# Local attention and two MoE layers in one kernel: a new offline order from a planner whose model of the loads, due times and dummies are changed

## The chip, the cores and the metric

The kernel runs on one core of a Trainium2 chip. The time is the device time of one execution in microseconds, as the median of several runs; lower is better.

## What is computed

Attention in 16 heads (2 batches, 8 heads, 576 positions, 64 wide), each head once on means of four positions and once in a narrow band, and then two layers without experts' routing: the first with a rational function between its two products, the second with h x tanh(softplus(h)), which is Mish.

```python
q_d = q.reshape(B, H, Sd, factor, D).mean(axis=3)        # k_d, v_d likewise; factor 4
out_up = np.repeat(sm_attn(q_d, k_d, v_d), factor, axis=2)
mask = np.abs(pos[:, None] - pos[None, :]) < factor
out_local = softmax(np.where(mask, scale * q @ k.T, -1e9)) @ v
x = (out_up + out_local) -> [1152, 512]
h = x @ w_in                                             # 512 -> 2048, weights in float64
g = (a0 + a1 h + a2 h^2 + a3 h^3) / (1 + |b0||h| + |b1| h^2 + 1e-6)
x = g @ w_out                                            # 2048 -> 512
h = x @ w_in2;  out = (h * tanh(softplus(h))) @ w_out2
```

## The kernel before

The instructions are issued in an order that the program works out while it is built. `Plan.add` takes tasks: the engine or engines that may run one, its cost in microseconds, a due value (`prio`), what it waits for, and the buffers it takes and uses. `Plan.run` then plays the engines forward in time. A free engine takes the ready task with the least due value whose buffers are free, and calls its function, which emits the instructions. So the due values and the costs set only the order in which each engine's instructions stand in its queue. On the chip each queue runs in order, and semaphores hold it where data are missing. A number in the planner is no time of the chip.

Attention is cut into 18 units of 128 query rows of a pair of heads (`unit`; the last of each batch takes windows of four pairs and is called mixed). A unit has these tasks: the q load (`qload`, due value less LOFF), the v loads of its windows (`vload` in `unit`, L665, four DMAs, eight for a mixed one, due value plus VOFF, two buffers `vw`), transposes of q (`pe_a`, L552 as a helper's line), masked scores (`pe_b`, L712 to L728), maxima and exponentials on VectorE and ScalarE, transposes of the probabilities (`pe_d`), the products with v (`pe_e`, L827 and L837), and the writing of x as a high and a low part (`xhi`, `xlo`). Before the first unit of a pair of heads comes `prep`, with the k load (due value less KOFF), the load of v for the means (due value plus VROFF, L614), transposes, and sums on VectorE and POOL (L603, L620, L624). The units' due values start at PROL and rise by PSTEP in the first chunk; later chunks lie LEAD ahead of the layer's work that needs them; UOFF adds a number to each of the 18.

Weights come as 32 pieces ("grains") of 1 MB in float64, through two buffers `raw`. Their load (L994 for w_in, L999 for w_out) is due LLEAD ahead of use, their conversion CLEAD ahead: two ScalarE passes (L1011, L1018), a join on VectorE (L1025), a rounded high part (L1037) and a low part (L1042). OLAG puts the w_out pieces of the first layer later; GOFF adds a number to each of the first 12. The two small loads of a and b (L483, L484) have the fixed due value -34. All loads go through SP's queue, in the planned order.

The layers' work is done in steps of two blocks of 128 of the 2048 columns: products with w_in (L1155), the rational function (L1175 to L1254), products with w_out (L1288 in the first layer, L1290 in the second, whose first products are L1469 and L1525). The first group of the first layer works on chunks of 256, 256, 256 and 384 tokens, so that it can start when the first attention units are done.

Where TensorE has nothing ready in the planner, `fill` puts in a dummy product on zeros (`warm`, L533, 480 columns), if the share of work that the planner counts in a short look-back is under FILL. It occupies TensorE in the plan. It is emitted only while the plan's time lies in SHOW; outside, the plan leaves a hole of the same length. The planner models a load by the time that its issue takes on SP, at most eight at once, then 0.3 us, then its moving time behind the loads before it, then 1.1 us.

Of the kernel before, what the change touches and what calls it, by code (L numbers as in the profile page):

```python
# [25 lines left out]

SECOND = 1.8
COLD, FILL_ALL = 3.4, 20
WINDOW, FILL, FILL_END = 3.4, 0.9, 450.0
SHOW = (2.4, 30.0)  # L30
LEAD, CLEAD, LLEAD, OLAG = 38, 14, 40, 18
PROL, PSTEP, VOFF, VROFF, LOFF, KOFF = -45, 2.5, 2, -1, 7, 9
GROUPS = ([6, 6, 4], [4, 4, 4, 4])
KCUT, MIX = 4, (1, 4)
MKP = -45
# [3 lines left out]
NRAW, NWT, NRING, NRING2 = 2, 2, 3, (2, 1)  # L39
LAT = {"pe": 0.2, "act": 0.16, "dve": 0.15, "pool": 0.15, "sp": 1.1}  # L40
QUEUED = 8
UOFF = [-3.0, 0.0, 0.0, 3.0, 4.5, 3.0, 3.0, -1.5, 6.0, 0.0, 0.0, -4.5, -4.5, 4.5, 6.0, 4.5, -1.5, -1.5]
GOFF = [0.0, 0.0, 0.0, 0.0, -4.0, -4.0, -10.0, -6.0, 2.0, -4.0, 10.0, 12.0]
HP = 15


# [34 lines left out]
class Plan:  # L81
# [6 lines left out]
    def add(self, engs, fn, prio, after=(), take=(), use=(), chain=None, dens=0.5, port=False, dma=(), sub=None):  # L88
        t = Task()
        t.dma, t.sub = dma, sub  # L90
        t.port = port
        t.dens = dens
        t.engs, t.fn, t.prio, t.take = engs, fn, prio, list(take)
        t.out, t.next, t.started, t.ended, t.seq = [], None, False, False, len(self.tasks)
        t.use = list(take) + list(use)
        deps = set(after)
        for b in take:
            b.owner = t
        for b in use:
            deps.add(b.owner)  # L100
        for b in t.use:
            b.users += 1
        deps.discard(None)
        t.deps = len(deps)
        if chain is not None:
            if chain in self.last:
                self.last[chain].next = t
                t.deps += 1
            self.last[chain] = t
        for d in deps:  # L110
            d.out.append(t)
        self.tasks.append(t)
        return t

    def run(self, names):
# [3 lines left out]
        landed, moved = [0.0] * QUEUED, 0.0  # L119
# [15 lines left out]
        def free(s):  # L135
            freed.setdefault(s.space, {})[s.lo, s.hi] = now
# [11 lines left out]
        def place(t, e):  # L148

            for k in banks(t):  # L150
                if any(f != e and end > now + 1e-6 for f, end in touched.get(k, {}).items()):
                    return False
            got = []
            for b in t.take:
                for s in sorted(b.slots, key=age):
                    used = live.setdefault(s.space, {})
                    if s.gate is not None and not s.gate.ended:
                        continue
                    if any(f != e and end > now + 1e-6 for k in s.banks for f, end in touched.get(k, {}).items()):
                        continue  # L160
                    if all(s.hi <= o.lo or o.hi <= s.lo for o in used.values()):
                        b.slot = s
                        used[id(b)] = s
                        got.append(b)
                        break
                else:
                    for g in got:
                        del live[g.slot.space][id(g)]
                        g.slot = None
                    return False  # L170
            return True

        def fill():
# [7 lines left out]
            for s in slots:  # L181
                used = live.setdefault(s.space, {})
                if all(s.hi <= o.lo or o.hi <= s.lo for o in used.values()):
                    b = Buf(slots)
                    b.slot, b.users, used[id(b)] = s, 1, s
                    if SHOW[0] <= now < SHOW[1]:
                        shown = fns[-1](s.view)
# [8 lines left out]
        while True:  # L196
            for e in names:
                if until[e] > now:
                    continue
                held = []  # L200
                while ready[e]:
                    item = heapq.heappop(ready[e])
                    t = item[2]
                    if t.started:
                        continue
                    one = next(iter(t.engs))
                    if e != one and until[one] + t.engs[one] <= now + t.engs[e] + SECOND:
                        held.append(item)
                        continue
                    if not place(t, e):  # L210
                        held.append(item)
                        continue
                    t.started = True
                    t.fn(e) if len(t.engs) > 1 else t.fn()
                    begin = max(now, 0.65) if e == "sp" else now
                    if e == "pool" or e == "dve" and t.port:

                        begin = max(now, port[0])
                        port[0] = begin + t.engs[e]
                    end = until[e] = begin + t.engs[e] * (2 if e == "pe" and now < COLD else 1)  # L220
                    there = end + LAT[e]
                    if t.dma:
                        end = begin
                        for issue, move in t.dma:
                            end = max(end, landed[-QUEUED]) + issue
                            moved = max(moved, end + 0.3) + move
                            landed.append(moved + LAT["sp"])
                        until[e], there = end, landed[-1]
                    n += 1
                    heapq.heappush(events, (end, n, 0, e, t))  # L230
                    heapq.heappush(events, (there, n, 1, e, t))
                    for k in banks(t):
                        touched.setdefault(k, {})[e] = there
                    if t.next is not None:
                        t.next.deps -= 1
                        if not t.next.deps:
                            enable(t.next)
                    if e == "pe":
                        busy.append((now, end, t.dens))
                    break  # L240
                for item in held:
                    heapq.heappush(ready[e], item)
                if e == "pe" and until[e] <= now:
                    got = fill()
                    if got:
                        b, dur = got
                        end = until[e] = now + dur * (2 if now < COLD else 1)
                        busy.append((now, end, 1))
                        n += 1
                        heapq.heappush(events, (end, n, 2, e, b))  # L250
            if not events:
                break
            now = events[0][0]
            while events and events[0][0] <= now + 1e-9:
                _, _, kind, e, t = heapq.heappop(events)
                if kind == 0:
                    if e == "pe":
                        release(t, e, True)
                    continue
                if kind == 2:  # L260
                    del live[t.slot.space][id(t)]
                    continue
                t.ended = True
                done += 1
                for b in t.use:
                    b.users -= 1
                    if not b.users:
                        del live[b.slot.space][id(b)]
                        free(b.slot)
                release(t, e, False)  # L270
# [4 lines left out]
def kernel(  # L275
# [26 lines left out]
    add = plan.add  # L302
# [184 lines left out]
    t_id = add({"pool": 1.1}, lambda: make_identity(nc, ident), -1000)  # L487
    t_m = add({"dve": 0.1}, lambda: nc.vector.memset(band, 0.0), -1900)
    t_cd = add({"dve": 0.6}, zeros, -1000)
    add({"dve": 0.4}, lambda: None, -880)  # L490
    t_bn = add({"pool": 0.5}, bands, -900, after=[t_m])
    def mask_set(lo, hi, ws):
        for w in ws:
            masks(*w)
# [2 lines left out]
    t_mk = [  # L497
        add({"dve": cost}, lambda x=x: mask_set(*x), pr, after=[t_bn])
        for cost, pr, x in (
            (0.4, -890, (0, 4, ((0, 0, 1), (0, 1, 1), (0, 2, 1), (0, 3, 1)))), (0.25, MKP, (3, 7, ((1, 4, 4),))),  # L500
            (0.25, MKP, (7, 11, ((2, 8, 4),))),
        )
    ]
    t_bias = add({"pool": 0.1}, biases, -20)
# [129 lines left out]
    def unit(u, slots, start):  # L634
        bb, kind, wins, prio, nw, n = u.bb, u.kind, u.wins, u.prio, NW, 32 * NW
        pairs = sorted({p for p, _ in wins})
        mixed = len(pairs) > 1
# [68 lines left out]
        def pe_b():  # L706
# [24 lines left out]
                        )  # L731

        tb = add(
            {"pe": 1.6 if mixed else 0.86}, pe_b, prio,
            after=tq + [kv_done[p] for p in pairs] + [t_i16, t_mk[kind]],
            take=[sc, tm, s, pd],
            use=[qT] + mix, chain="pb",
# [157 lines left out]
    first = [(0, 256), (256, 256), (512, 256), (768, 384)]  # L895
# [57 lines left out]
    for c in range(4):  # L953
        for i, (bb, kind, p) in enumerate(need[c]):
            if c == 0:
                prio = PROL + PSTEP * i
            else:
                prio = cstart[c - 1] + (i / len(need[c])) * (cstart[c] - cstart[c - 1]) - LEAD
            prio += UOFF[len(att_order)]
            att_order.append(prio)  # L960
# [20 lines left out]
    for g in sorted(grains, key=lambda g: grains[g]):  # L981
        m, kind, f = g
        pr = grains[g] + (GOFF[len(W)] if len(W) < len(GOFF) else 0.0)
        r, t, w = Buf(raw_s), Buf(wt_s), Buf(ring_s[kind])
# [600 lines left out]
```

## Time and profile before

| what | value |
|---|---|
| median of 3 runs | 481.8 us (479.96 to 482.65) |
| the profiled execution: its time, and the span of its instructions | 481.31 us, 479.5 us |
| busy share of the span: TensorE, VectorE, ScalarE, POOL | 98%, 79%, 70%, 12% |
| mean granted clock of TensorE | 0.993 of full speed |
| loads and stores | 47.17 MB, 98 GB/s in the mean |
| instruction packets on queue 8 | 32, 0.52 MB, 0.5% of the time of 16 DMA engines |

The profile is of one execution. Busy time of an engine is the time covered by its instructions; a TensorE matmul overlaps the next one, so the step between two is shorter than the duration shown. Idle time is put down to what ended it. The granted clock is a share of full speed, and has two levels, 1.2 and 2.4 GHz.

### The profile page before, as it was taken

Reading aid. Unit: us, or ns where it says so; the run is one execution under the profiler, and the core shown is the slowest. Engines: PE = TensorE matmul, PEld = TensorE weight load, DVE = VectorE, ACT = ScalarE, POOL = GpSimd, SP = SyncE. Lnnn points to the kernel's source line nnn. Section 1 sums busy time; section 2 is a strip of 40 time slices with the busy share of each in tenths; the row PEclk is TensorE's granted clock in tenths of the full one; section 3 lists DMA queues with packets and bytes.
Section 4 is the critical chain, followed back from the end, with each engine's and each line's share of the span. In section 5 each row is a group of like instructions: output and inputs, shape, how many; then the busy total and the mean of one; then the engine's idle time right before and its main releaser. Section 6 shows DMA issues by size and latency. Waiting matters only on the chain.

```text
span 479.5 us, 9855 instructions
## 1 busy us (share of the span) xinstructions
PE 467.6 (98%) x4081; PEld 428.5 (89%) x4081; DVE 376.8 (79%) x566; ACT 337.6 (70%) x529; POOL 58.7 (12%) x80
## 2 busy tenths in 40 slices
PE   8999898999999999999999999999999999999996
PEld 4667797889999999999999998898989898989885
DVE  6688789899899978997999989988596669524342
ACT  5778698885988799998878797578667446422320
POOL 2654345653000000000000000000000000000000
PEclk9999799999999999999999999999999999999999
DMA  8967976611422402333022022134314220000103
GB/s 180 234 172 176 263 184 182 153 42 36 168 89 90 143 34 87 106 130 117 0 89 89 1 89 87 45 115 143 137 21 156 87 89 0 1 0 2 66 1 131
DMA packets 45757, 47.17 MB, mean 98 GB/s; under 512 B 30352, under 2 KB 31120, under 8 KB 45712
## 3 DMA queue, kind: packets, MB, share of 16 engines
q1 hardware_dynamic: 45712, 46.54, 33.4%
q8 instruction: 32, 0.52, 0.5%
q14 instruction: 13, 0.11, 0.1%
HBM read 44.17 MB, written 2.36 MB: 97 GB/s over the span
## 4 chain that ended last, share of the span: by engine, by line
PE 74%; DVE 12%; DMA 8%; ACT 3%; issue 1%; SPq 1%; ACTq 0%
PE psum L1290 19%; PE psum L1155 18%; PE psum L1288 15%; PE psum L1469 11%; PE psum L1525 5%; DMA att<-in_q_dram 3%; DMA raw<-in_moe_w_in_dram 3%; PE psum L837 1%; DMA att<-in_v_dram 1%; PE psum L827 1%; DVE wt L1025 1%; PE psum L552 1%; DVE xl L1311 1%; DVE wrk L1329 1%; PE psum L728 1%
## 5 line engine op out<-in xcount | busy, mean ns | idle before, releaser
L1155 PE MATMUL psum<-xh,wi 128*128 128x384 f32 (+1 forms) x336 | 84.7, 323 | 0.2 <-DVE wrk L1184 0.2
L1288 PE MATMUL psum<-gg,wo 128*128 128x384 f32 (+1 forms) x480 | 76.2, 313 | 0.0
L1288 PEld LDWEIGHTS psum<-gg,wo 128*128 128x128 f32 x480 | 72.8, 189 | 0.5 <-issue 0.2
L1155 PEld LDWEIGHTS psum<-xh,wi 128*128 128x128 f32 x336 | 60.2, 193 | 1.5 <-issue 0.9
L1155 PE MATMUL psum<-xl,wi 128*128 128x384 f32 (+1 forms) x168 | 53.1, 316 | 0.0
L1290 PE MATMUL psum<-wo,gg 128*128 128x512 f32 x216 | 51.7, 391 | 0.0
L1290 PE MATMUL psum<-wo,late_g 128*128 128x512 f32 x216 | 51.3, 391 | 0.0
L1290 PEld LDWEIGHTS psum<-wo,late_g 128*128 128x128 f32 x216 | 40.4, 188 | 8.0
L1290 PEld LDWEIGHTS psum<-wo,gg 128*128 128x128 f32 x216 | 40.4, 188 | 8.0
L1025 DVE SCALAR_TENSOR_TENSOR wt<-wt,raw 128x1024 int32<-128x1024 int32 x32 | 40.4, 1266 | 7.5 <-ACT wt L1011 6.5
L1011 ACT ACTIVATE wt<-raw 128x1024 f32<-128x1024 f32 x32 | 36.4, 1137 | 8.7 <-DVE wo L1042 4.8
L1018 ACT ACTIVATE raw<-raw 128x1024 int32<-128x1024 uint16 x32 | 36.8, 1149 | 4.7 <-DMA raw<-in_moe_w_out_dram 3.4
L1525 PE MATMUL psum<-xh,wi 128*128 128x384 f32 x128 | 34.5, 335 | 0.0
L1155 PEld LDWEIGHTS psum<-xl,wi 128*128 128x128 f32 x168 | 32.5, 193 | 0.0
L1401 DVE TENSOR_TENSOR part<-psum,part 128x512 f32<-128x512 f32 x27 | 17.8, 687 | 13.6 <-PE psum L1290 13.6
L1155 PE MATMUL psum<-xh,late_r 128*128 128x384 f32 x96 | 25.5, 334 | 0.0
L1175 ACT ACTIVATE wrk<-psum 128x768 f32<-128x768 f32 (+1 forms) x27 | 19.9, 735 | 6.6 <-PE psum L1155 6.0
L1037 ACT ACTIVATE wo<-wt 128x1024 fp32r<-128x1024 f32 x11 | 11.7, 1061 | 17.7 <-DVE wt L1031 7.7
L1042 DVE TENSOR_TENSOR wo<-wt,wo 128x1024 fp32r<-128x1024 f32 x14 | 17.1, 1218 | 8.7 <-ACT wo L1037 8.7
L1525 PEld LDWEIGHTS psum<-xh,wi 128*128 128x128 f32 x128 | 23.3, 188 | 0.2
L1099 ACT ACT_TABLE_LOAD x17 | 21.8, 1283 | 0.3
L1525 PE MATMUL psum<-xl,wi 128*128 128x384 f32 x64 | 21.4, 335 | 0.0
(164 smaller groups left out, 1038.5 us busy)
## 6 DMA issues: line engine op xcount, KB each, us to landing
raw<-in_moe_w_in_dram SPq DMA_DIRECT2D x16, 1024.0 KB, 5.4
raw<-in_moe_w_out_dram SPq DMA_DIRECT2D x16, 1024.0 KB, 4.9
att<-in_v_dram SPq DMA_DIRECT2D x72, 48.0 KB, 4.0
out_dram<-part SPq DMA_DIRECT2D x9, 256.0 KB, 2.0
att<-in_q_dram SPq DMA_DIRECT2D x16, 128.0 KB, 3.9
att<-in_k_dram SPq DMA_DIRECT2D x6, 288.0 KB, 3.8
att<-in_v_dram SPq DMA_DIRECT2D x6, 288.0 KB
wrk<-in_k_dram SPq DMA_DIRECT2D x2, 288.0 KB, 6.2
```

The source lines that it names most:

```text
L1011: nc.scalar.activation(out=t.v, in_=words(r)[:, :, 1].bitcast(F32), func=AF.Prelu if fold else AF.Identity, scale=2.0 ** -112, **({"alpha" ...
L1018: nc.scalar.activation(out=words(r)[:, :, 0], in_=r.v.bitcast(U16).rearrange("p (n four) -> p n four", four=4)[:, :, 1], func=AF.Copy, sca ...
L1025: nc.vector.scalar_tensor_tensor(out=ti, in0=ti, scalar=3, in1=words(r)[:, :, 0], op0=ALU.logical_shift_left, op1=ALU.bitwise_or)
L1042: ENG[e].tensor_tensor(out=w.v[:, 1], in0=s.v, in1=w.v[:, 0].bitcast(F32), op=ALU.subtract)
L1099: nc.scalar.preload_act_table_set(name)
L1155: nc.tensor.matmul(st.h.v[:, i, :T], w.v[:, ww, ks], xx[:, kk, c0:c0 + T], start=(nn == 0 and (st.big or i == 0)), stop=(nn == 3 * KD - 1 ...
L1175: nc.scalar.activation(out=vw(st.a), in_=H(), func=AF.Square)
L1288: nc.tensor.matmul(A(d)[:, :T], w.v[:, ww, lo + d * 128:lo + (d + 1) * 128], vw(gg)[:, i, :], start=start, stop=stop)
L1290: nc.tensor.matmul(A(d), vw(gg)[:, i, sl], w.v[:, ww, lo:lo + DM], start=start, stop=stop)
L1401: nc.vector.tensor_tensor(out=pv, in0=acc.v[:, j], in1=pv, op=ALU.add)
L1469: nc.tensor.matmul(dst.v[:, :TW], wv.v[:, ww, at:at + 128], x(h, kk), start=bool(take) and nn == 0, stop=nn == 5, skip_group_check=not take,)
L1525: nc.tensor.matmul(h.v[:, i, :TW], w.v[:, ww, at:at + 128], xx[:, kk, c0:c0 + TW], start=nn == 0, stop=nn == 3 * KD - 1)
```

## The change

Only numbers that go into the planner change, and one term in its model of the loads. The functions that emit instructions are the same, except that dummies are emitted over a longer part of the plan.

- The model of a load's moving time gets a term: for each 7.0 us of the time line of moved data that a load crosses, 0.8 us more (FETCH).
- SHOW goes from (2.4, 30) to (2.4, 450): every dummy in the plan from 2.4 us on is emitted. FILL goes from 0.9 to 0.7, after the first 20 us.
- Due values: CLEAD, LLEAD, OLAG, PSTEP, VROFF, LOFF, and the lists UOFF and GOFF.
- Task costs of the bands, the masks and the scores products; an empty VectorE task is dropped.

```diff
--- before.py
+++ after.py
@@ -26,10 +26,9 @@
 
 SECOND = 1.8
 COLD, FILL_ALL = 3.4, 20
-WINDOW, FILL, FILL_END = 3.4, 0.9, 450.0
-SHOW = (2.4, 30.0)
-LEAD, CLEAD, LLEAD, OLAG = 38, 14, 40, 18
-PROL, PSTEP, VOFF, VROFF, LOFF, KOFF = -45, 2.5, 2, -1, 7, 9
+WINDOW, FILL, FILL_END = 3.4, 0.7, 450.0
+LEAD, CLEAD, LLEAD, OLAG = 38, 20, 30, 26
+PROL, PSTEP, VOFF, VROFF, LOFF, KOFF = -45, 3.0, 2, 2, 5, 9
 GROUPS = ([6, 6, 4], [4, 4, 4, 4])
 KCUT, MIX = 4, (1, 4)
 MKP = -45
@@ -39,8 +38,10 @@
 NRAW, NWT, NRING, NRING2 = 2, 2, 3, (2, 1)
 LAT = {"pe": 0.2, "act": 0.16, "dve": 0.15, "pool": 0.15, "sp": 1.1}
 QUEUED = 8
-UOFF = [-3.0, 0.0, 0.0, 3.0, 4.5, 3.0, 3.0, -1.5, 6.0, 0.0, 0.0, -4.5, -4.5, 4.5, 6.0, 4.5, -1.5, -1.5]
-GOFF = [0.0, 0.0, 0.0, 0.0, -4.0, -4.0, -10.0, -6.0, 2.0, -4.0, 10.0, 12.0]
+FETCH = (0.8, 7.0)
+SHOW = (2.4, 450.0)
+UOFF = [1.5, 0.0, 1.5, 9.0, 13.5, 13.5, 6.0, 18.0, 13.5, 9.0, 3.0, -6.0, -7.5, -3.0, 9.0, 12.0, -7.5, -7.5]
+GOFF = [0.0, 2.0, 8.0, 4.0, 0.0, -4.0, -4.0, -22.0, 18.0, 0.0, -6.0, 24.0]
 HP = 15
 
 
@@ -223,7 +224,8 @@
                         end = begin
                         for issue, move in t.dma:
                             end = max(end, landed[-QUEUED]) + issue
-                            moved = max(moved, end + 0.3) + move
+                            first = max(moved, end + 0.3)
+                            moved = first + move + FETCH[0] * (int((first + move) / FETCH[1]) - int(first / FETCH[1]))
                             landed.append(moved + LAT["sp"])
                         until[e], there = end, landed[-1]
                     n += 1
@@ -487,8 +489,7 @@
     t_id = add({"pool": 1.1}, lambda: make_identity(nc, ident), -1000)
     t_m = add({"dve": 0.1}, lambda: nc.vector.memset(band, 0.0), -1900)
     t_cd = add({"dve": 0.6}, zeros, -1000)
-    add({"dve": 0.4}, lambda: None, -880)
-    t_bn = add({"pool": 0.5}, bands, -900, after=[t_m])
+    t_bn = add({"pool": 1.0}, bands, -900, after=[t_m])
     def mask_set(lo, hi, ws):
         for w in ws:
             masks(*w)
@@ -497,8 +498,8 @@
     t_mk = [
         add({"dve": cost}, lambda x=x: mask_set(*x), pr, after=[t_bn])
         for cost, pr, x in (
-            (0.4, -890, (0, 4, ((0, 0, 1), (0, 1, 1), (0, 2, 1), (0, 3, 1)))), (0.25, MKP, (3, 7, ((1, 4, 4),))),
-            (0.25, MKP, (7, 11, ((2, 8, 4),))),
+            (0.8, -890, (0, 4, ((0, 0, 1), (0, 1, 1), (0, 2, 1), (0, 3, 1)))), (0.5, MKP, (3, 7, ((1, 4, 4),))),
+            (0.5, MKP, (7, 11, ((2, 8, 4),))),
         )
     ]
     t_bias = add({"pool": 0.1}, biases, -20)
@@ -731,7 +732,7 @@
                         )
 
         tb = add(
-            {"pe": 1.6 if mixed else 0.86}, pe_b, prio,
+            {"pe": 1.52 if mixed else 0.78}, pe_b, prio,
             after=tq + [kv_done[p] for p in pairs] + [t_i16, t_mk[kind]],
             take=[sc, tm, s, pd],
             use=[qT] + mix, chain="pb",
```

## Rows read from the trace of the kernel before

**Rows 1.** Stretch, length, busy us of PE, PEld, DVE, ACT, POOL; clock, DMA share, GB/s

```profile
0.00:30.00 30.00, 27.89 (x458) 16.84 (x462) 21.65 (x72) 20.50 (x55) 15.52 (x30) 1.00 0.94 212
30.00:60.00 30.00, 27.57 (x559) 23.86 (x559) 24.20 (x58) 21.91 (x59) 12.66 (x16) 0.89 0.81 197
60.00:90.00 30.00, 28.15 (x526) 25.32 (x525) 27.83 (x58) 26.76 (x58) 16.32 (x18) 1.00 0.73 189
90.00:122.00 32.00, 31.27 (x627) 28.09 (x626) 29.18 (x61) 23.85 (x62) 14.12 (x18) 1.00 0.28 67
122.00:300.00 178.00, 178.00 (x1049) 176.72 (x1049) 163.68 (x181) 155.82 (x178) 0.11 (x1) 1.00 0.25 85
```

**Rows 2.** All dummies: least, median and most ns, first and last start, form

```profile
L533 PE MATMUL psum<-blank x61: 365/366/607, 1.2 to 30.7; 128*128 128x480 bf16 x61
```

**Rows 3.** Timeline of TensorE, 25 to 31 us: start, length, line, work, count

```profile
25.75 1.59 PE L533 MATMUL psum<-blank 128*128 128x480 bf16 x7
...
29.95 0.26 PE L712 MATMUL psum<-mask,eye 64*32 64x192 bf16 x4
...
30.73 0.38 PE L533 MATMUL psum<-blank 128*128 128x480 bf16 x1
30.77 0.46 PE L1155 MATMUL psum<-xh,wi 128*128 128x256 f32 x1
```

**Rows 4.** Chain of work that ended last, 28 to 60 us: start, length, what

```profile
40.35 0.72 PE psum L1155 x6
...
43.68 0.60 PE psum L837 x32
...
47.81 4.65 DMA att<-in_v_dram
...
52.51 1.03 PE psum L837 x30
...
54.21 1.33 PE psum L1155 x6
```

**Rows 5.** Waits, 30 to 122 us: us in total, times, longest (TensorE; SP's queue)

```profile
PE psum L837 <- DMA att<-in_v_dram: 1.5, 1, 1.5
PE psum L552 <- ACT att L593: 1.1, 1, 1.1
...
SPq L665 <- PE psum L837: 16.0, 8, 5.4
```

**Rows 6.** Stretches of 2 us around the wait at 51 us

```profile
48.00:50.00 2.00, 2.00 (x26) 1.99 (x19) 1.85 (x5) 1.71 (x6) 0.30 (x1) 1.00 0.94 215
54.00:56.00 2.00, 2.00 (x32) 1.78 (x34) 1.00 (x2) 1.76 (x4) 0.35 (x1) 0.50 1.06 358
58.00:60.00 2.00, 2.00 (x13) 2.00 (x13) 1.78 (x4) 0.87 (x5) 0.00 (x0) 0.64 0.58 105
```

**Rows 7.** Loads, 45 to 60 us: packets, MB, share; by line, median landing us

```profile
q8 instruction: 2, 0.03, 1.0%
...
raw<-in_moe_w_out_dram SPq DMA_DIRECT2D x2, 1024.0 KB, 8.3
```

**Rows 8.** Loads of the whole span by line: count, KB each, median landing us

```profile
att<-in_v_dram SPq DMA_DIRECT2D x72, 48.0 KB, 4.0
```

**Rows 9.** Timeline of SP's issues: start, length on SP, line, load

```profile
15.37 0.51 SPq L994 DMA_DIRECT2D raw<-in_moe_w_in_dram  x1
...
23.74 1.65 SPq L483 DMA_DIRECT2D a_sb<-in_moe_a_dram  x1
25.43 1.17 SPq L484 DMA_DIRECT2D b_sb<-in_moe_b_dram  x1
...
48.34 0.91 SPq L999 DMA_DIRECT2D raw<-in_moe_w_out_dram  x2
```

**Rows 10.** Timeline of VectorE, 29 to 84 us: weight low part, weight join

```profile
29.67 1.21 DVE L1042 TENSOR_TENSOR wi<-wt,wi 128x1024 fp32r<-128x1024 f32 x1
...
63.64 1.21 DVE L1025 SCALAR_TENSOR_TENSOR wt<-wt,raw 128x1024 int32<-128x1024 int32 x1
```

## Prediction

> **What bounds the kernel now.** I read the busy time by stretches first [rows 1]. From 122 us to 300 us TensorE is busy 178.00 of 178 us at full clock; up to the end only the change of stage near 305 us and the last few microseconds leave it idle. So the second part is a fixed amount of TensorE work, and the change leaves that work alone. What an order can win or lose lies before 122 us. There I find three kinds of waste.
>
> First, idle time: 2.11 us before 30 us, then 2.43, 1.85 and 0.73 us, 5.01 us together between 30 and 122 us [rows 1]. Second, dummies: 61 of them stand between 1.2 and 30.7 us, and seven back to back take 1.59 us and a single one 0.37, so one more costs (1.59 - 0.37)/6 = 0.20 us and all of them about 12.4 us [rows 2, 3]. They fill time in which attention or the first weights are not ready, and cost nothing as long as that holds. Third, one stretch at a lower clock. A quarter of a unit's v load is issued at 47.81 us and lands after 4.65 us, and the product on it goes on only at 52.51 us [rows 4]; the list of waits gives 1.5 us for it, the longest TensorE wait between 30 and 122 us [rows 5]. After the wait the granted clock is 0.50, that is 1.2 GHz, the lower of its two levels; before it TensorE was busy without a gap, and from 58 to 60 us the clock averages 0.64, so the low level lasts to about 59.4 us [rows 6]. Six 256-column matmuls take 1.33 us there against 0.72 us at full clock; 30 of the v products take 1.03 us against 0.60 us for 32 [rows 4]. That is a factor of about 1.8. The slow stretch is about 6.9 us (52.5 to 59.4), so 6.9 x (1 - 1/1.8) = 3.1 us is lost, and the event costs 1.5 + 3.1 = **4.6 us**.
>
> In the same time VectorE is busy 24.20, 27.83 and 29.18 us of 30, 30 and 32 [rows 1]. It is close to a bound of its own between 60 and 122 us, which limits what a better order can win there.
>
> **The change part by part.** The code of every task stays; only the order list, and so the in-order queue of each engine, is new.
>
> *Instruction packets in the planner's model (FETCH).* It issues nothing. It charges 0.8 us for each 7.0 us in which loads move. The trace has such packets: in the 15 us around the event two, 0.03 MB together and 1.0% of the time of 16 engines, so 0.010 x 15 x 16 / 2 = 1.2 us each, and one per 7.5 us [rows 7]. The assumption is near what is seen. The median v quarter lands in 4.0 us [rows 8], the one that stalled in 4.65 us [rows 4]: 0.65 us late, about one packet. The old model puts such a landing at 0.3 + 0.33 + 1.1 = 1.7 us after issue when nothing is queued, so even with a packet the new one stays some 1.5 us short of 4.0 us. The correction points the right way and is smaller than the error.
>
> The Trainium skill, "DMA: Bandwidth & Descriptors", section "Queues, rings and completion order", says that an engine alternates between its queue rows and drains a whole packet before it switches; the late quarter agrees with that. Its page "Runtime: NRT & Kernel Launch", section "Instruction fetch mechanics", speaks against the change: it calls the cost of a block boundary mostly hidden. By that rule the term of 4.6 us below is zero; I give it a rival.
>
> *Event at 51 us.* The v loads sit in two buffers, and SP waits 16.0 us in eight places for the products that free them [rows 5]. The load can't be issued sooner; what can change is which products TensorE puts between. With the landing planned later, I expect this wait to be covered: -4.6 us. Bounds: -4.6 (gone) and 0 (it turns up at another of the 18 units). I take -4.6, since the planner now sees part of the delay, and after a covered wait the next late thing is the 1.1 us wait for a ScalarE copy [rows 5], which cost no clock.
>
> *All dummies after 2.4 us, not only those before 30 us.* A dummy in the queue costs 0.20 us if real work stands ready behind it, nothing if TensorE would wait anyway. How many there will be the trace can't show. Counted from the list of before by its own planner, 19 hidden ones come after 30 us, most of them in places at 60 to 80 us; FILL 0.7 for 0.9 asks for fewer. Bounds: nothing to 19 x 0.20 = 3.9 us; a gain is possible only where a planned idle place is also a real one and the clock would have fallen. In the trace TensorE stands idle 1.85 us between 60 and 90 us [rows 1], which covers about nine of them. I take half of the rest: (19 - 9)/2 x 0.20 = 1.0 us.
>
> *a and b loads.* Their due value stays at -34, while the first w_in load goes from -40 to -30. So they pass ahead of it. Their two issues hold SP 1.65 and 1.17 us in the trace, in a full queue, from 23.74 us; the first w_in is issued at 15.37 us in 0.51 us [rows 9], and the load of the fifth unit's q, which now comes after it, gives some of that back. Bounds 0 to 2.8 us. Behind it waits the first product: the last piece of its weight is made on VectorE from 29.67 us, and the product starts at 30.77 us, with no gap to hide in [rows 3, 10]. I take +0.6 us: two issues as short as the w_in's own would be 1.0 us, less what the q load gives back.
>
> *Due times of weights and attention.* Weight loads of the first group get due values later by 10 (w_in, first), 12, 18, and 22, 22, 18 (w_out), attention units by -7.5 to +19.5, mostly +3 to +10 among the first ten. Relative to attention, the w_out loads move back by some 10 to 20 units. The first two w_out loads go together from 48.34 us [rows 9] and land 8.3 us after issue in the middle [rows 7], at about 57 us; the join of the first on VectorE, at 63.64 us [rows 10], comes some 7 us later. That cover hides a delay of 7 us; beyond it every microsecond delays the first output products. Conversions get due values earlier by 6, so they pass attention work on ScalarE and VectorE; this shifts waits between the two and removes no VectorE work. The pair loads of v (VROFF) come 3 later and pass q and weight loads on SP; POOL's additions wait behind them. I cost these together at 0, bounds -2 to +3 (less than the 5.01 us of idle in that stretch, either way).
>
> *Task costs.* The scores products of a unit take 30.73 - 29.95 = 0.78 us [rows 3]; the planner had 0.86 and gets 0.78. The first masks had 0.4 and an empty VectorE task of 0.4 behind them and get 0.8, the same sum. Figures in a list, no work moved by themselves: 0.
>
> **Sum.** -4.6 + 1.0 + 0.6 = -3.0 us. The profiled execution took 481.31 us (span 479.5), half a microsecond under the median of 481.8. 481.3 - 3.0 = **478.3 us**. A measurement of this kernel can tell about 0.5%, 2.4 us, from no change: faster means under 479.4, slower over 484.2.
>
> **The rivals.**
>
> *The stall moves (0.20).* Each of the 18 units has a v load in two buffers, and the planner still thinks that it lands more than a microsecond too early. Another one then stalls and takes the clock with it: event 0, 481.3 + 1.6 = 482.9 us. For it: the 16.0 us of buffer waits on SP. Against: only one of 18 stalled TensorE in before.
>
> *The packets don't matter (0.10).* If they hide behind the issue, the planner has learnt nothing, and the order is another draw of the same quality: 482.9 us too, between 479.4 and 486. For it: they are 1% of DMA time. Against: 4.65 us beside 4.0 us. (This is what the runtime page says of fetching.)
>
> *Weights come too late (0.25): slower.* The w_out loads move behind attention loads on SP, and these wait for buffers. From 7 us of delay on, the first output products wait; TensorE's queue is in order, so it stands 1.5 us, as for the v load, to twice that, and the clock falls as at 51 us, 3.1 us more. One such event besides the old one: 481.3 + 1.6 + 4.6 to 6.1 = 487.5 to 489 us; if the old one is gone, 482.9 to 484.4. For it: relative shifts of 10 to 20. Against: the loads are issued by a planner that puts products where their weights are due.
>
> **How the numbers follow.** The forecast has 0.45: event gone, 473 to 479.4 with the bounds of the other terms. The rivals have 0.20, 0.10 and 0.25. Faster by over 0.5%: the forecast and a sliver of the draws, 0.47. Within: the first two rivals and the mild end of the third, 0.25. Slower: the rest, 0.28. The range goes from 473 us (481.3 - 4.6 - 2 with no dummy in the way, and 1.7 us of the 12.4 us of early dummies no longer needed) to 488 us (the near end of the bad case).
>
> **What would show it.** Right: no stretch at the lower clock between 30 and 122 us; idle time there under 4 us; TensorE saturated from about 119 us; dummies after 30 us, some 10 to 20, with little ready behind them. Wrong: a TensorE wait of over a microsecond on a v or weight load with clock 0.50 after it; the first w_in product well after 31 us; the join of the first w_out later than 64 us with TensorE idle. The prediction fails above all if the planner's v landing is still too early where it hurts, or if the prologue before 30 us, of which I forecast no change, gets shorter or longer by itself.

## The result, and the profile after

| | before | after |
|---|---|---|
| median of 22 runs each, side by side | 480.10 us (477.18 to 483.14) | 482.16 us (480.79 to 484.65) |
| ratio | 1 | 1.0054, interval 1.0034 to 1.0073 |
| the profiled execution: time, span | 481.31, 479.5 us | 483.62, 481.8 us |
| mean granted clock in it | 0.993 | 0.996 |

The change makes the kernel slower by 0.54%, about 2 us. A second comparison, with one of the experiments (12 runs against 17), gave 482.15 against 478.94 us, ratio 1.0063 [1.0035, 1.0091]. Lines of the changed kernel are one higher than before: L533 is L534, L1155 is L1156.

The stretches of after, as in [rows 1] (stretch, length, busy us of PE, PEld, DVE, ACT, POOL, clock, DMA share, GB/s):

```profile
0.00:30.00 30.00, 27.66 (x452) 16.34 (x452) 20.29 (x70) 19.26 (x52) 14.06 (x29) 1.00 0.79 177
30.00:60.00 30.00, 27.63 (x568) 21.29 (x565) 26.69 (x61) 23.69 (x61) 10.84 (x16) 0.98 0.88 199
60.00:90.00 30.00, 30.00 (x535) 26.05 (x533) 26.54 (x59) 25.30 (x58) 17.39 (x19) 0.96 0.64 156
90.00:122.00 32.00, 31.82 (x628) 29.05 (x627) 31.18 (x57) 24.82 (x58) 13.44 (x17) 1.00 0.49 138
122.00:300.00 178.00, 178.00 (x1059) 177.17 (x1059) 164.38 (x182) 154.92 (x179) 1.20 (x1) 1.00 0.25 83
```

Up to 60 us TensorE is as busy as before. Then the order does what I had hoped for: 30.00 of 30 and 31.82 of 32 us, where before had 28.15 and 31.27. The idle time from 30 to 122 us is 2.55 us against 5.01. By busy time alone this kernel ought to be ahead, but busy time counts dummies. The summary of all dummies of after, as in [rows 2]:

```profile
L534 PE MATMUL psum<-blank x96: 363/366/608, 1.2 to 63.2; 128*128 128x480 bf16 x96
```

There are 96, the last at 63.2 us, where before had 61 up to 30.7 us. From 30 to 65 us stand 35, where before had 2. The timeline of TensorE (start, length, line, work) shows how the stretch begins:

```profile
30.23 1.78 PE L534 MATMUL psum<-blank 128*128 128x480 bf16 x8
...
34.07 0.39 PE L1156 MATMUL psum<-xh,wi 128*128 128x256 f32 x1
```

Eight dummies in a row, and the first product with w_in at 34.07 us; in [rows 3] it is at 30.77. The waits of TensorE from 30 to 122 us, as in [rows 5], and the 2-us stretches around the longest:

```profile
PE psum L798 <- ACT att L813: 1.0, 1, 1.0
PE psum L721 <- issue: 0.7, 1, 0.7
PE psum L729 <- DVE att L604: 0.7, 1, 0.7
```

```profile
54.00:56.00 2.00, 1.45 (x43) 0.89 (x41) 2.00 (x5) 1.23 (x2) 0.00 (x1) 1.00 1.02 322
56.00:58.00 2.00, 0.85 (x12) 0.54 (x12) 2.00 (x5) 2.00 (x5) 0.00 (x0) 1.00 1.32 144
58.00:60.00 2.00, 2.00 (x45) 1.43 (x43) 2.00 (x5) 2.00 (x8) 0.00 (x0) 0.69 1.28 178
60.00:62.00 2.00, 2.00 (x47) 0.96 (x44) 0.78 (x4) 1.97 (x3) 0.87 (x2) 0.50 1.28 187
62.00:64.00 2.00, 2.00 (x16) 1.05 (x14) 1.69 (x4) 0.84 (x4) 0.17 (x1) 0.96 0.96 153
```

The 1.5 us wait on a v load is gone. In its place come a wait for ScalarE and one for VectorE, and after 1.70 us idle of 4 the granted clock goes to 0.69, 0.50 and 0.96. The lacking shares, 2 x 0.31 + 2 x 0.50 + 2 x 0.04 = 1.7 us at full speed, are 3.4 us at the lower level, against 6.9 before.

SP's timeline of after (start, length on SP, load), for [rows 9]:

```profile
13.53 0.36 SPq L485 DMA_DIRECT2D a_sb<-in_moe_a_dram  x1
13.94 0.43 SPq L486 DMA_DIRECT2D b_sb<-in_moe_b_dram  x1
15.99 2.89 SPq L666 DMA_DIRECT2D att<-in_v_dram  x4
...
19.58 0.64 SPq L995 DMA_DIRECT2D raw<-in_moe_w_in_dram  x1
...
22.98 6.39 SPq L666 DMA_DIRECT2D att<-in_v_dram  x8
30.11 0.39 SPq L995 DMA_DIRECT2D raw<-in_moe_w_in_dram  x1
...
34.67 7.33 SPq L666 DMA_DIRECT2D att<-in_v_dram  x8
...
45.95 0.38 SPq L995 DMA_DIRECT2D raw<-in_moe_w_in_dram  x1
```

The a and b loads take 0.36 and 0.43 us, not 1.65 and 1.17. The first w_in load goes at 19.58 us, not 15.37, behind v loads that wait for their buffers (15.99 us, 2.89 us long). The second goes at 30.11, the third at 45.95 us. Eight v loads, which hold SP for 7.33 us with their issues and waits, stand between those two. The second and third of the kernel before:

```profile
23.21 0.47 SPq L994 DMA_DIRECT2D raw<-in_moe_w_in_dram  x1
...
32.93 0.40 SPq L994 DMA_DIRECT2D raw<-in_moe_w_in_dram  x1
```

### The profile page after: what moved, and what is told of

Same layout as the page of the kernel before. It is cut to its first block, busy times and chain, and to the rows that moved or that the text cites. A ratio compares the mean times of both kernels' runs of the same rounds, so it can differ in the third digit from the quotient of the medians.

```text
span 481.8 us, 9927 instructions
## 1 busy us (share of the span) xinstructions
PE 472.2 (98%) x4116; PEld 429.5 (89%) x4116; DVE 381.3 (79%) x567; ACT 339.1 (70%) x528; POOL 56.9 (12%) x80
## 4 chain that ended last, share of the span: by engine, by line
PE 77%; DVE 15%; ACT 5%; issue 2%; DMA 1%; POOL 0%; SPq 0%; ACTq 0%; POOLq 0%
PE psum L1291 18%; PE psum L1156 17%; PE psum L1289 15%; PE psum L1470 11%; PE psum L1526 5%; PE psum L534 2%; PE psum L838 2%; PE psum L828 1%; PE psum L553 1%; PE psum L721 1%; DVE wt L1026 1%; PE psum L729 1%; DMA att<-in_q_dram 1%; DVE xl L1312 1%; DVE wrk L1330 1%
## 5 line engine op out<-in xcount | busy, mean ns | idle before, releaser
L1156 PE MATMUL psum<-xh,wi 128*128 128x384 f32 (+1 forms) x336 | 83.2, 319 | 0.0
L1156 PEld LDWEIGHTS psum<-xh,wi 128*128 128x128 f32 x336 | 58.9, 189 | 0.9 <-issue 0.5
L1156 PE MATMUL psum<-xl,wi 128*128 128x384 f32 (+1 forms) x168 | 52.4, 312 | 0.0
L1012 ACT ACTIVATE wt<-raw 128x1024 f32<-128x1024 f32 x32 | 36.3, 1138 | 4.3 <-DVE late_r L1079 1.7
L1526 PE MATMUL psum<-xh,wi 128*128 128x384 f32 x128 | 34.2, 335 | 0.0
L1156 PEld LDWEIGHTS psum<-xl,wi 128*128 128x128 f32 x168 | 31.8, 189 | 0.0
L534 PE MATMUL psum<-blank 128*128 128x480 bf16 x96 | 25.3, 391 | 1.2 <-DVE band L490 1.2
L1156 PE MATMUL psum<-xh,late_r 128*128 128x384 f32 x96 | 25.3, 334 | 0.0
L1526 PEld LDWEIGHTS psum<-xh,wi 128*128 128x128 f32 x128 | 23.3, 188 | 0.2
L1038 ACT ACTIVATE wo<-wt 128x1024 fp32r<-128x1024 f32 x12 | 12.7, 1059 | 15.3 <-PE psum L1291 5.4
L1536 ACT ACTIVATE wrk<-psum 128x768 f32<-128x768 f32 x7 | 5.7, 814 | 24.6 <-PE psum L1526 24.6
L1043 DVE TENSOR_TENSOR wo<-wt,wo 128x1024 fp32r<-128x1024 f32 x14 | 18.1, 1297 | 5.7 <-ACT wo L1038 5.5
```

Of the source, the lines that this page charges most:

```text
L534: nc.tensor.matmul(view[:, :480], blank[:, :128], blank, start=True, stop=True)
L1012: nc.scalar.activation(out=t.v, in_=words(r)[:, :, 1].bitcast(F32), func=AF.Prelu if fold else AF.Identity, scale=2.0 ** -112, **({"alpha" ...
L1043: ENG[e].tensor_tensor(out=w.v[:, 1], in0=s.v, in1=w.v[:, 0].bitcast(F32), op=ALU.subtract)
L1156: nc.tensor.matmul(st.h.v[:, i, :T], w.v[:, ww, ks], xx[:, kk, c0:c0 + T], start=(nn == 0 and (st.big or i == 0)), stop=(nn == 3 * KD - 1 ...
L1526: nc.tensor.matmul(h.v[:, i, :TW], w.v[:, ww, at:at + 128], xx[:, kk, c0:c0 + TW], start=nn == 0, stop=nn == 3 * KD - 1)
```

## The experiments

All kernels keep the work and the functions that emit it. Only the order, or the number of dummies, differs.

**Is the event at 51 us a property of the order?** The kernel before once more, unchanged:

> The kernel before, unchanged, for a second profile and more times. If the wait at 51 us belongs to the order, it is there again with the lower clock behind it. If it comes from how the loads happen to fall, it may be gone, and that execution is nearer to 477.5 us than to 481.

It took 479.49 us, ratio 1.0018 [0.9989, 1.0047]. Its profiled execution (477.7 us, span 475.9) has no wait on a load from 30 to 122 us. Its stretches of 2 us at the event's place, and of 10 us later (columns as above):

```profile
50.00:52.00 2.00, 2.00 (x51) 1.75 (x50) 1.93 (x6) 1.97 (x6) 1.43 (x3) 1.00 1.04 408
52.00:54.00 2.00, 2.00 (x55) 1.64 (x55) 2.00 (x6) 1.92 (x6) 1.39 (x3) 1.00 1.02 410
70.00:80.00 10.00, 8.14 (x138) 6.94 (x140) 9.93 (x19) 9.55 (x21) 5.25 (x6) 1.00 0.73 200
80.00:90.00 10.00, 8.87 (x179) 7.87 (x179) 8.22 (x21) 7.55 (x17) 6.32 (x8) 1.00 0.62 162
```

TensorE is busy throughout at full clock from 50 to 54 us. What is left is 1.86 and 1.13 us of idle time from 70 to 90 us. So the list does not bring the event in every execution.

Then a cover for it. Eight dummies ahead of the products that had waited, in the same list:

```diff
+        at = [i for i, x in enumerate(listed) if x[1] == "pe_e"][7]
+        listed[at:at] = [("pe", "dummy", None, lambda: warm(warm_s[0].view))] * 8
```

> The kernel before with eight dummies (1.6 us) put into TensorE's queue ahead of the products with v that waited 1.5 us at 51 us and lost the clock; all else the same. If the event costs what I reckoned, the wait stays but the clock holds: 3.1 us less than before, about 477 us, in executions that have the wait. If VectorE's load between 60 and 110 us takes the gain back: within 1 us of 480.1, with more TensorE idle time between 70 and 100 us. If the wait is not there in most executions: up to 1.6 us more.

479.06 us, ratio 1.0000 [0.9975, 1.0025]. The cover neither gains nor costs, within 1.2 us either way, and the 477 us that I had expected with an ordinary event did not come. Nor does it hold the clock: 8 of its 12 executions have a mean granted clock of 0.996 or lower.

How much the loss of clock is worth over many executions can be read from the runs themselves, since each has its mean granted clock. All runs of the kernel before that have one, and all of the changed kernel:

| mean granted clock | before: runs, median | after: runs, median |
|---|---|---|
| 0.999 or 1.000 | 27 of 100, 478.5 us | 27 of 34, 481.9 us |
| 0.996 to 0.998 | 35, 478.7 us | 6, 483.7 us |
| 0.995 or lower | 38, 480.7 us | 1, 484.7 us |
| all | 479.1 us | 482.2 us |

The changed order keeps the clock in 27 of 34 executions, the order before in 27 of 100; what keeps it there is taken up below, with the dummies. But the executions of the first row, called undisturbed from here on, are only 0.6 us below the median of before (479.1 - 478.5), and 1.1 us in the means, not 4.6. That counts every loss of clock, wherever in the execution it falls. And with next to no loss of clock the changed order is 3.4 us longer (481.9 - 478.5).

**Where do these microseconds go?** The changed kernel again, so that two executions with next to no loss of clock can be laid side by side:

> The changed kernel itself beside the three runs above, as their base: 1.003 to 1.007 of the kernel before. In its new profile the products with w_in between 30 and 65 us should be 40 to 60 again and the third w_in load should be issued after 42 us; if not, the starvation was an accident of one execution as the wait at 51 us was in the kernel before.

482.15 us. The profiled execution (482.39 us, span 480.6, clock 1.000) has the same stretch with few w_in products, so that is no accident of one execution. First the kernel before, second execution, then the changed kernel, second execution: stretches 0 to 30, 30 to 65 and 65 to 122 us, then TensorE's products with w_in from 30 to 65 us alone, then the dummies there.

```profile
0.00:30.00 30.00, 27.50 (x447) 16.87 (x448) 20.82 (x71) 19.71 (x53) 14.60 (x28) 1.00 0.92 210
30.00:65.00 35.00, 35.00 (x735) 30.75 (x733) 31.46 (x74) 32.32 (x79) 18.17 (x21) 1.00 0.88 218
65.00:122.00 57.00, 53.42 (x1011) 48.05 (x1009) 51.97 (x109) 44.63 (x106) 26.76 (x32) 1.00 0.48 131
```

```profile
30.00:65.00 35.00, 17.98 (x120) 15.31 (x120) 1.00 0.88 218
```

```profile
L533 PE MATMUL psum<-blank x6: 366/366/376, 29.7 to 32.0; 128*128 128x480 bf16 x6
```

```profile
0.00:30.00 30.00, 27.87 (x427) 16.70 (x430) 18.95 (x70) 18.81 (x51) 13.54 (x28) 1.00 0.80 175
30.00:65.00 35.00, 33.02 (x732) 24.87 (x721) 31.03 (x71) 28.90 (x74) 15.02 (x21) 1.00 0.83 193
65.00:122.00 57.00, 56.81 (x1047) 52.14 (x1047) 54.50 (x106) 46.36 (x107) 28.07 (x33) 1.00 0.53 147
```

```profile
30.00:65.00 35.00, 8.40 (x53) 6.91 (x54) 1.00 0.83 193
```

```profile
L534 PE MATMUL psum<-blank x35: 363/366/377, 30.8 to 61.9; 128*128 128x480 bf16 x35
```

Products with w_in fall from 120 (17.98 us) to 53 (8.40 us). Dummies rise from 4 to 35 (of the six listed, two start before 30 us). Dummies at 0.20 us [rows 2, 3] taken off, TensorE does 35.00 - 0.8 = 34.2 us of work in that stretch before, and 33.02 - 7.0 = 26.0 after: 8.2 us less. From 65 to 122 us it does 56.81 against 53.42, 3.4 us more. The first 30 us (27.87 with 61 dummies against 27.50 with 57) are 0.4 us less. The sum is 5.2 us lost, and the spans differ by 480.6 - 475.9 = 4.7. The working that a prediction needed was this one: how much real work is there for TensorE in each stretch.

**Are the dummies the loss, or what fills it?** The changed order with the dummies after 30 us left out again:

```diff
-SHOW = (2.4, 450.0)
+SHOW = (2.4, 30.0)
```

> The changed kernel with its order as it is, but the 35 dummies behind 30 us not emitted; the order of every engine is otherwise the same. Theory A (the new order brings ready work to TensorE later, and the dummies only fill the waits): 481 to 484 us, as the changed kernel (482.2); the idle time of TensorE between 30 and 122 us rises from 3.3 us by some 5 to 7 us, and the clock may fall more often. Theory B (the added dummies stand in front of ready work): 35 x 0.20 = 7 us less at most, 476 to 479 us, idle time unchanged.

485.27 us, ratio 1.0133 [1.0099, 1.0168]: slower than the changed kernel by another 3 us. Two stretches of it:

```profile
40.00:50.00 10.00, 8.58 (x191) 6.45 (x189) 8.35 (x21) 7.87 (x22) 2.76 (x5) 0.83 0.67 152
60.00:70.00 10.00, 9.71 (x133) 8.63 (x133) 7.65 (x17) 7.40 (x18) 5.80 (x8) 0.50 0.75 139
```

The granted clock falls to 0.83 and then to 0.50 for ten microseconds. That is about 3.4 and 10 us at the lower level, against 3.4 us with the dummies. At the factor 1.8 [rows 4] this is 10 x 0.44 = 4.4 us more lost; idle time from 30 to 70 us goes from 2.37 to 5.55 us, 3.2 more; and 30 dummies, 6.1 us, are saved. That makes about +1.5 us; the spans of the two profiled executions differ by 483.7 - 481.8 = 1.9. Theory A has the sign, but the time lies over its 481 to 484 us, and the idle time from 30 to 122 us rose by 3.1 us, not by 5 to 7. So most of these dummies stand where TensorE has nothing else, and pay. They also keep the clock: all six executions without them have a lowered one (0.981 to 0.991), in the same order. That later planned landings keep it is not shown. The same lines in the order before (its 19 hidden dummies emitted):

> The kernel before with its order as it is, but with the 19 dummies that its plan has behind 30 us emitted too. Theory A: within 1 us of the kernel before (480.1), since they stand where the plan expects TensorE to wait; a little less if the clock holds better. Theory B: up to 19 x 0.20 = 3.9 us more, 482 to 484 us.

479.18 us, ratio 1.0008 [0.9984, 1.0032]: no difference.

**Is it the late w_in loads?** First through the due values. In the changed planner the first three w_in loads get their due values of before, and in the planner of before the later ones of the change (the second edit is the same with -30.0, -22.2, -10.5):

```diff
-        x = add({"sp": 0.5}, load, pr - LLEAD, ...
+        x = add({"sp": 0.5}, load, {(0, "i", 0): -40.0, (0, "i", 1): -34.2, (0, "i", 2): -28.5}.get(g, pr - LLEAD), ...
```

> The changed kernel, planned anew with one thing undone: the due values of the first three w_in loads are those of before (-40, -34.2, -28.5 for -30, -22.2, -10.5). Theory W (the later w_in loads starve TensorE between 30 and 65 us): the third conversion begins before 45 us instead of 55 us, and the time is 478 to 480 us. Theory R (numbers and model were fitted to each other, and any order off that point is worse, whichever part is touched): no gain, 482 to 487 us, although the third load is early.

> The kernel before, planned anew with the later due values of the first three w_in loads alone (-30, -22.2, -10.5). Theory W: 2 to 4 us slower than before, 481 to 484 us, with TensorE idle between 40 and 65 us. Theory R: slower by any amount, with the idle time anywhere.

The late loads in the planner of before: 491.95 us, ratio 1.0232 [1.0169, 1.0294], 11 us slower where Theory W had 2 to 4. Its w_in products from 30 to 65 us:

```profile
30.00:65.00 35.00, 3.82 (x24) 3.10 (x24) 0.84 0.83 212
```

The early loads in the changed planner: 485.29 us, ratio 1.0109 [1.0067, 1.0152]. Its w_in products from 30 to 65 us, and the stretch from 150 to 300 us:

```profile
30.00:65.00 35.00, 15.70 (x96) 12.63 (x96) 1.00 0.79 175
```

```profile
150.00:300.00 150.00, 148.50 (x847) 146.69 (x846) 137.22 (x150) 128.98 (x144) 0.00 (x0) 1.00 0.23 78
```

The w_in products are back, and the kernel is still slower, since the rest of the list was planned anew: 19 dummies from 64.7 to 96.9 us and 1.5 us idle behind 150 us, where the order had neither. So a due value can't be tested alone: each edit draws another list. The due lines exchanged as a whole say the same. Due lines of the change in the planner of before, and those of before in the planner of the change:

> The kernel before with the changed due values alone (the five lines of leads and offsets), without the term for packets, the new task costs and the added dummies. Theory W: the late loads come with the due values, so 482 to 485 us. Theory R: also worse than before, 482 to 487 us. If the packet term is what harms: as before, 479 to 481 us.

> The changed kernel with the due values of before: packet term, task costs and all dummies alone. Theory W: as before or a little better, 477 to 480 us. Theory R: 482 to 487 us.

487.92 us, ratio 1.0159 [1.0116, 1.0202], and 485.62 us, ratio 1.0112 [1.0066, 1.0157]. Each half of the change alone comes out slower than the whole in the median. Their w_in products from 30 to 65 us are 99 and 105, so neither is short of them, and both are slower for other reasons, which these runs don't separate. The cost of a single line, task costs among them, can't be read from them either.

Then with the list frozen: the changed kernel's order is written out, and only the third w_in piece's own steps are moved (467 is its load, 468 to 472 its conversion, 727 to 734 its products). The first run moves its load, the second also its conversion and eight of its products into the places of eight dummies, the third also the steps behind these. behind(x, y) puts task x right behind task y:

```diff
+        behind(467, 202)
+        behind(468, 174)
+        behind(469, 468)
+        behind(470, 205)
+        behind(471, 698)
+        behind(472, 699)
+        at = listed.index(entry[701])
+        holes = [x for x in shown if listed.index(x) > at][:8]
+        for what, hole in zip(range(727, 735), holes):
+            listed.remove(entry[what])
+            listed[listed.index(hole)] = entry[what]
+        behind(735, 214)
...
```

> The changed kernel's own list, with one entry moved: the load of the third w_in piece stands on SP behind the second v load after the second piece's, so it should be issued near 35 us and not at 45.95 us. Nothing else moves. If the load itself is what is late, its conversion (55.30 us) starts sooner and the time falls by 1 to 3 us against the changed kernel. If the conversion's place in ScalarE's queue is what holds it, the conversion still starts near 55 us and the time is the same within 1 us. If loads moved ahead of v loads cost attention more, it gets slower by 1 us or more.

> As the run before, and the conversion of the third piece moved too (ScalarE passes near 45 us, join near 47 us), and its first eight products put in the places of eight dummies near 46 to 50 us; the eight dummies are gone. If the late piece makes the loss: TensorE has 8 x 0.20 = 1.6 us less to do in 30 to 65 us, so 1 to 2 us less than the changed kernel. If VectorE or the attention steps set the pace there, the same time within 0.5 us, with the idle time of TensorE up by what the dummies took. If the conversion passes attention work that TensorE waits for, slower by 1 us or more.

> As the run before, and the first steps behind these eight products (two ScalarE copies, two VectorE steps) moved up as well, so that the rational function of the step isn't left where it was. If the late piece makes the loss: 1.5 to 3 us less than the changed kernel, and not more than the run before. If it doesn't: within 0.5 us of the changed kernel or slower.

The load alone: 485.72 us, ratio 1.0127 [1.0082, 1.0172], 3.6 us slower than the order it came from. Its row on SP and the one behind it, the wait of TensorE, that q load in the chain of work that ended last (start, length), and ScalarE's conversion of the piece (L1016 is L1012 in the changed kernel):

```profile
41.84 0.40 SPq L999 DMA_DIRECT2D raw<-in_moe_w_in_dram  x1
42.29 0.67 SPq L653 DMA_DIRECT2D att<-in_q_dram  x1
```

```profile
PE psum L557 <- DMA att<-in_q_dram: 2.9, 1, 2.9
```

```profile
42.29 5.87 DMA att<-in_q_dram
```

```profile
58.13 0.63 ACT L1254 ACTIVATE gg<-wrk 128x512 fp32r<-128x512 f32 x1
58.67 1.15 ACT L1016 ACTIVATE wt<-raw 128x1024 f32<-128x1024 f32 x1
```

And ScalarE in the changed kernel at the same place:

```profile
53.08 0.47 ACT L594 ACTIVATE att<-psum 128x288 f32<-128x288 f32 x1
54.77 0.63 ACT L1250 ACTIVATE gg<-wrk 128x512 fp32r<-128x512 f32 x1 [1.22 <-DVE wrk L1224]
55.30 1.12 ACT L1012 ACTIVATE wt<-raw 128x1024 f32<-128x1024 f32 x1
```

The load was issued at 41.84 us and not, as I had expected, near 35 us. The conversion began no sooner, 17 us after the issue, right behind ScalarE's work before it: its place in ScalarE's queue holds it, not the data. And the 1 MB now stood right ahead of a q load that landed 5.9 us after its issue, and for which TensorE waited 2.9 us. In the changed kernel the same q load is issued at 42.06 us, and the transposes on it start at 45.26 us without a wait, so it has landed within 3.2 us. With the conversion moved too it is worse: 492.82 and 492.24 us, ratios 1.0272 [1.0234, 1.0311] and 1.0286 [1.0235, 1.0338]. ScalarE's and TensorE's longest single waits, the same in both runs:

```profile
ACT wt L1016 <- DMA raw<-in_moe_w_in_dram: 3.0, 1, 3.0
```

```profile
PE psum L557 <- ACT att L687: 4.8, 1, 4.8
```

I had put the conversion before its data, so ScalarE stood 3.0 us, and the copy of q behind the two passes of the conversion made TensorE wait 4.8 us. These two runs refute my placing, not the idea that an earlier piece would help; that it would is not shown.

**Are the packets in the planner worth something?** All numbers of the changed planner were fitted anew, by the end of its plan, twice with the packet term and twice without (this line for the second two; LEAD to KOFF, UOFF, GOFF and three smaller numbers, MKP, SUMS and HP, differ in all four, and FILL is 0.7, 0.6, 0.8 and 0.5):

```diff
-FETCH = (0.8, 7.0)
+FETCH = (0.0, 7.0)
```

> The changed kernel's planner as it is, packet term and all dummies, but its due values and offsets fitted anew (a search that lowers the plan's own end by 1.4 units, from the changed kernel's numbers). The work is the same. Theory P (the model with packets is a good guide, the changed kernel's numbers were only not fitted far enough): below the changed kernel by 1 to 3 us, 479 to 481 us. Theory N (the packet term misleads: it plans slack that the chip then runs through as dummies): no better than the changed kernel, 481 to 485 us, whatever the fit.

> As the run before, fitted from the due values of the kernel before (0.7 units below the changed kernel's plan). Theory P: 480 to 482 us. Theory N: 481 to 485 us.

> The changed kernel's planner without the packet term, all dummies emitted, due values and offsets fitted with the same effort. Theory P: the plan is too hopeful about the loads, so TensorE waits more between 30 and 65 us, and 481 to 486 us. Theory N: the weights stand earlier in the queues, the second and third conversion before 42 us, and 476 to 480 us.

> As the run before, from a second search that ended 2.5 units higher. Theory P: 482 to 487 us. Theory N: 478 to 482 us.

| | median | ratio to before |
|---|---|---|
| with packets | 481.25 us | 1.0036 [1.0013, 1.0058] |
| with packets, second | 481.28 us | 1.0043 [1.0023, 1.0063] |
| without | 482.48 us | 1.0053 [1.0025, 1.0082] |
| without, second | 482.60 us | 1.0069 [1.0042, 1.0095] |

The two with packets lie 1.2 to 1.3 us lower. The intervals overlap, and there are two fits on each side, whose other numbers differ too; it points to a small gain and doesn't settle it. The 476 to 482 us that Theory N had for the two without did not come. Undisturbed are 12 and 9 of 12 executions with the term, 9 of 13 and 1 of 12 without. None reaches the order before. The third conversion of a w_in piece, at 53.01 us in the first and at 37.42 us in the third of these, doesn't order them, and neither do the w_in products from 30 to 65 us: 73, 90, 105 and 53. Their lateness alone doesn't set the end.

## Why the prediction was wrong

*The event at 51 us (-4.6 us): mis-sized, the largest error.* The wait was read rightly. But a wait with a lowered clock behind it is a chance event of an execution: the next execution of the same list has none there. All losses of clock together are worth 0.6 us in the median and 1.1 us in the mean. I charged the whole loss of one execution, and took it for an ordinary one since it lay within half a microsecond of the median of three runs, 481.8 us. Those three lay high: the median is 480.1 us of the 22 side by side and 479.1 us of the 100 in the table, and with its clock of 0.993 the profiled execution belongs to the lowest row, 38 of 100. The mechanism isn't borne out either. The changed order keeps its clock with the help of the dummies, which I had counted as a cost, and that it covered this wait can't be told from profiles, since one of the kernel before lacks the wait too. The rule of the Trainium skill that stood against the term ("Runtime: NRT & Kernel Launch", section "Instruction fetch mechanics", mostly hidden) came nearer, with 0, than I did; no run shows which of the late landings are due to packets.

The reading of the late quarter was weak as well. I held its 4.65 us against the 4.0 us of the whole span and called it one packet late. The v loads around it, in the view of [rows 7], take longer than it did:

```profile
att<-in_v_dram SPq DMA_DIRECT2D x8, 48.0 KB, 7.3
```

*Due times (0, bounds -2 to +3): the loss that I put at nothing.* I wrote down that the w_in loads become due 10, 12 and 18 later, and then weighed only the w_out loads, since these had 7 us of cover that I could read. For w_in I had the opposite in hand: a first product that starts as soon as its weight is there, "with no gap to hide in". What the new list costs is 8.2 us of work from 30 to 65 us, of which 3.4 come back by 122 us. With the early stretch that is 5.2 us by this count, 4.7 us in the spans of two undisturbed executions, and 3.4 us between medians of such executions. The bound of +3 had come from the idle time of before, and idle time doesn't bound what can be lost: missing work appears as dummies. That the due values alone put the loss there is not shown. Late w_in values take the w_in products away in the planner of before (24 left), and early ones bring them back in that of the change (96), but with all due values of the change the planner of before has 99. The loss belongs to the list as a whole.

*Dummies (+1.0, 0 to 3.9): wrong sign for the new order.* I counted 19 in the list of before. The new list has 35 after 30 us, all before 64 us; without them it is 3 us slower. They are the mark of the loss and not its cause.

*a and b loads (+0.6): passed ahead of the first w_in load, as forecast.* Their issues take 0.8 us; what they cost the end no run shows. The first w_in load was held by v loads ahead of it, whose buffers were not free.

*Packets in the model, task costs (0).* Packets: some 1.2 us between the fits, unsettled. Task costs: never alone, open.

*The rivals.* "Weights come too late" was the nearest, with 482.9 to 484.4 us if the event is gone. Its place was wrong: w_in and not w_out, and not as one stall but as a stretch filled with dummies. The join of the first w_out piece moved from 63.64 to 67.92 us, within the cover of 7 us. "The stall moves" came about in another form in the profiled execution: the waits before the lowered clock are for ScalarE and VectorE, not for a v load, and the loss is smaller (3.4 us at the lower level against 6.9). The second execution has none. What I had named as signs stood there: the first w_in product well after 31 us, and dummies after 30 us beyond 20. What stays open is which entries of the list set the end. The edits of due values and single entries that were tried cost some 3 to 11 us each, whichever way they went.

## What to carry to other kernels

Before a stall in a profile is priced, look at it in a second execution, or at the spread of times and clocks over the runs; a wait on a load is worth its mean, not its worst. For a new order, count useful work by stretch, with fillers taken off, and follow the first weights of the next stage: here the first product stood right behind its weight. Fillers that stand in real holes are not the loss, and taking them out can cost the clock as well. In a list made by a planner one value is no local edit: in-order queues pass each delay on, and a large load moved ahead can make the small load behind it late.

## What the runs showed of the hardware

The same list gives different executions: 476.4 to 484.0 us over 100 runs of the kernel before, with mean granted clocks from 0.984 to 1.000. A wait of 1.5 us on a load in one execution is absent in the next.

The clock did not follow idle time in a simple way. From 70 to 80 us the kernel before is idle for 1.86 us in its second execution (shown above), and the clock stays at full speed. With the eight dummies at 51 us, in the same order otherwise, it is idle for 1.85 us there, and the clock falls:

```profile
70.00:80.00 10.00, 8.15 (x107) 6.84 (x105) 9.67 (x18) 9.19 (x21) 5.09 (x5) 0.83 0.71 190
```

The place of the loss changes too. In the profile of the kernel before with its hidden dummies the clock is at 0.56 from 20 to 30 us and at 1.00 from 30 to 122 us.
